# A third working tile for decoding packed weights on ScalarE, VectorE and GpSimd, in an FFT convolution with two MLP layers

## The chip, the cores and the metric

The kernel runs on one core of one Trainium2 chip. The metric is the device time of one execution in microseconds (us); for a set of runs, their median.

## What is computed

The input `x` (2 x 3008 x 256) is filtered along its 3008 time steps in the frequency domain, and the 6016 tokens that come out pass through two feed-forward layers, all in float32 accuracy:

```
X = np.fft.rfft(x, axis=1)
y = np.fft.irfft(X * (filt_r + 1j * filt_i)[None], n=3008, axis=1)
x = y.reshape(6016, 256)
g = x @ w_gate;  x = ((g / (1 + np.exp(-g))) * (x @ w_val)) @ w_out      # d_ff 1536
h = x @ w_in;    out = (h * np.clip(h + 3, 0, 6) / 6) @ w_out2           # d_ff 2048
```

The weights of the layers arrive as 64-bit words (`w1`, `w2`, the arrays `w_in` of the trace). The kernel itself turns them into float32, with integer and float operations on the two 32-bit halves of each word: this is the decoding.

## The kernel before

After the convolution the tokens are worked on in six blocks of up to 1024, each as two half blocks of 512 (or 480) columns. Layer 1 needs twelve units of work for a block (`F1` = 12), layer 2 eight (`G2` = 8). The main loop (`for s in range(S)`) runs over units: first the units of layer 1 for blocks 1 to 5, then those of layer 2 for all blocks. Matmuls of the first product of a unit write the banks `gv` (line 654); those of the second product, which need `hs`, write the banks `a` (line 699). In a unit of layer 1 TensorE executes 33 matmuls: seven products of three, and between them three groups of four of the second product of the unit before, which `fill()` hands out. Each float32 operand is split into a high part (a cast on ScalarE, line 687 for `hs`) and a low part (a subtraction on VectorE, line 116), and the second product multiplies those parts.

The order of instructions on every engine is the order in which the program writes them (`manual_schedule`). In a unit there are places, the spots N, A, B, T and C, at which extra work is put in by `add(unit, spot, step)`. So go:

- the weights of the unit after next: `split_unit` casts them on ScalarE (line 509) and subtracts on GpSimd (line 116, tiles `wu` and `wo`), from the stage tile `st`, which `ask_unit` loads (line 497);
- the next block's tokens: `plan_x` with loads `g` (line 141) or `raw` (line 740);
- the decoding of layer 2's weights, during layer 1's blocks 2 to 5: four steps q = 0 to 3 in each block, 16 in all, of 512 words a partition each.

A step of the decoding is an object of `Decode`. `ask_w2` loads its words into a tile `raw` (line 178) and `start` makes the tile `wa` with ScalarE's Abs of the high halves (line 183). `part` 0 to 4 run on VectorE (lines 192 to 202; part 1 makes the tile `ww`, part 4 is the last to read `raw`). `finish_w2` ends it on GpSimd: two additions of 256 columns (line 119), `ww` += `wa`, for every second step also four sums `sm`; one unit later the result goes to memory (lines 800 and 802). The places are dealt out of this list, five to a step, of which neighbours share one:

```
free_spots = [(u, name) for u in range(7) for name in "ABC" if (u, name) not in ((0, "B"), (1, "A"))]
...
places = [(s + u, name) for u, name in free_spots[4 * q:4 * q + 5]]
u, name = places[0]
add(u - 2, "N", ask_w2, g, i)
add(u - 1, "B", lambda g, i: dec2[g, i].start(), g, i)
```

The tiles of the decoding lie in the pool `late`, which has two buffers of a tag unless a tile asks for another number (`ww` asks for four). A tile of a tag takes over the place of the one that many allocations before it, and its first writer waits until the last user of that one is done. The pool is closed three units before layer 2 begins, and a pool of layer 2's tiles takes over its storage.

Of the kernel before, what the change touches and what calls it, by code (L numbers as in the profile page):

```python
# [9 lines left out]
F32 = mybir.dt.float32  # L10
# [6 lines left out]
P = 128  # L17
# [61 lines left out]
def fft_conv_glu_mlp(ctx: ExitStack, tc: tile.TileContext, x, filt, mats, sgn, w1, w2, out):  # L79
# [86 lines left out]
    class Decode:  # L166
# [12 lines left out]

        def start(self):  # L180
            if self.a is None:
                self.a = self.pool.tile([P, self.n], F32, tag="wa", name="wa")
            nc.scalar.activation(out=self.a, in_=self.raw[:, :, 1].bitcast(F32), func=AF.Abs)

        def part(self, i, engine=None):
# [77 lines left out]
    with tc.manual_schedule():  # L263
# [386 lines left out]
        def product(acc, s, a, i, start):  # L650
            k = units[s][0]
            n, w = half(k), wu[s][0]
            for q, (r, v) in enumerate(((0, 0), (0, 1), (1, 0))):
                nc.tensor.matmul(acc[:, :n], w[:, r, FORM[a] * P:(FORM[a] + 1) * P], xs_part(k, v, i),  # L654
                                 start=start and q == 0, stop=q == 2, skip_group_check=True)
# [160 lines left out]
        for k in range(2, n_block):  # L816
            s = F1 * (k - 1)
            for q in range(4):
                g, i = divmod(4 * (k - 2) + q, 2)
                places = [(s + u, name) for u, name in free_spots[4 * q:4 * q + 5]]  # L820
                u, name = places[0]
# [145 lines left out]
```

## Time and profile before

| | us |
|---|---|
| median of 3 runs | 1142.1 |
| lowest and highest run | 1141.64, 1144.41 |
| profiled execution | 1143.04 |
| its span, first to last instruction | 1141.2 |
| TensorE (PE) busy | 1119.2 (98%) |
| VectorE (DVE) busy | 853.5 (75%) |
| ScalarE (ACT) busy | 752.1 (66%) |
| GpSimd (POOL) busy | 598.0 (52%) |

The rows below are from the profiled execution. PEld is TensorE's loading of weights, which overlaps its matmuls; SPq is the queue of SyncE, which issues the DMAs. In a timeline a row may merge several instructions of a kind (x4); the time in brackets is how long the engine was idle before it, with the instruction that released it.

### The profile page before, as it was taken

To read this page: it belongs to the slowest core of one execution; us is meant where nothing else is said; L and a number is where in the kernel's file an instruction comes from. 1 tells how busy PE (TensorE), PEld (TensorE's weight loads), DVE (VectorE), ACT (ScalarE), POOL (GpSimd) and SP (SyncE) were. 2 spreads that over 40 slices of the span, in tenths; PEclk is the share of its full clock that TensorE was granted. 3 is DMA by queue.
4 is the path that set the end of the run, shared out by engine and by line. 5 is a ranking of instruction groups with operands and counts; after the bars stand their busy time and mean duration, and the time that the engine had idled before them with its cause. 6 is when DMAs were issued, how large, how long until landed. Compare 5 with 4: busy or idle time off the path is not lost.

```text
span 1141.2 us, 19170 instructions
## 1 busy us (share of the span) xinstructions
PE 1119.2 (98%) x7232; PEld 926.9 (81%) x7232; DVE 853.5 (75%) x1164; ACT 752.1 (66%) x1363; POOL 598.0 (52%) x779
## 2 busy tenths in 40 slices
PE   9999999999999999999999999999999999999998
PEld 7678887888788788878878888888888888888887
DVE  5889986668768777876877867768677677677765
ACT  4555447667567657756766777677677777777664
POOL 4752376755755765565567645444345444344440
PEclk9999999999999999999999999999999999999999
DMA  9964954732733462272354242322322412422200
GB/s 313 298 194 143 283 172 153 215 111 81 221 109 120 132 177 83 100 211 86 114 202 130 97 153 65 116 95 77 149 78 76 145 54 76 148 72 77 98 21 34
DMA packets 59484, 150.65 MB, mean 132 GB/s; under 512 B 5536, under 2 KB 27424, under 8 KB 57888
## 3 DMA queue, kind: packets, MB, share of 16 engines
q1 hardware_dynamic: 58848, 148.92, 40.4%
q8 instruction: 56, 0.92, 0.3%
q10 hardware_dynamic: 544, 0.52, 0.1%
q14 instruction: 36, 0.29, 0.1%
HBM read 117.17 MB, written 32.24 MB: 131 GB/s over the span
## 4 chain that ended last, share of the span: by engine, by line
PE 89%; DVE 3%; issue 2%; POOL 2%; DMA 2%; ACT 1%; SPq 1%; DVEq 0%
PE gv L654 42%; PE a L699 35%; PE gv L229 5%; PE a L237 2%; PE gv L370 1%; PE gv L156 1%; PE gv L328 1%; PE a L344 1%; POOL wu L116 1%; DMA ring<-x_in 1%; DVE h L681 1%; POOL ww L119 0%; DVE xs L116 0%; DMA w1f<-x 0%; DMA d<-turned 0%
## 5 line engine op out<-in xcount | busy, mean ns | idle before, releaser
L654 PE MATMUL gv<-xs,wu 128*128 128x512 f32 (+1 forms) x2268 | 572.2, 388 | 1.2 <-DVE h L593 0.8
L116 POOL TENSOR_TENSOR wu<-st,wu 128x224 fp32r<-128x224 f32 x432 | 311.6, 753 | 423.7 <-ACT wu L509 411.1
L654 PEld LDWEIGHTS gv<-xs,wu 128*128 128x128 f32 x2268 | 424.7, 189 | 87.7 <-DVE gv L119 3.4
L699 PE MATMUL a<-hs,wo 128*128 128x512 f32 (+1 forms) x1872 | 480.6, 387 | 10.4 <-ACT hs L687 10.4
L699 PEld LDWEIGHTS a<-hs,wo 128*128 128x128 f32 x1872 | 352.1, 188 | 79.1 <-ACT hs L687 12.6
L116 DVE TENSOR_TENSOR hs<-h,hs 128x1024 fp32r<-128x1024 f32 (+3 forms) x228 | 234.9, 1030 | 81.0 <-ACT hs L687 75.7
L687 ACT CAST hs<-h 128x512 fp32r<-128x512 f32 (+3 forms) x216 | 172.5, 799 | 132.2 <-DVE h L683 73.9
L116 POOL TENSOR_TENSOR wo<-st,wo 128x256 fp32r<-128x256 f32 x156 | 147.7, 959 | 0.0
L683 DVE SCALAR_TENSOR_TENSOR h<-h,gv 128x512 f32<-128x512 f32 (+1 forms) x144 | 96.4, 670 | 23.4 <-ACT h L677 23.0
L509 ACT CAST wu<-st 128x384 fp32r<-128x384 f32 x216 | 110.7, 563 | 0.6 <-DMA st<-w1f 0.6
L675 ACT ACTIVATE h<-gv 128x512 f32<-128x512 f32 (+1 forms) x120 | 70.6, 588 | 57.1 <-PE gv L654 56.8
L119 DVE TENSOR_TENSOR gv<-gv,h 128x512 f32<-128x512 f32 (+1 forms) x108 | 73.9, 685 | 43.7 <-PE gv L654 38.1
L677 ACT ACTIVATE h<-gv 128x512 f32<-128x512 f32 (+1 forms) x144 | 84.1, 584 | 16.2 <-PE gv L654 16.1
L119 DVE TENSOR_TENSOR h<-gv,h 128x512 f32<-128x512 f32 (+1 forms) x108 | 72.9, 675 | 25.7 <-PE gv L654 25.4
L862 ACT COPY gv<-gv 128x512 f32<-128x512 f32 (+1 forms) x108 | 60.9, 564 | 42.7 <-PE gv L654 39.1
L683 DVE SCALAR_TENSOR_TENSOR h<-h,h 128x512 f32<-128x512 f32 (+1 forms) x48 | 32.7, 681 | 59.4 <-ACT h L677 59.4
L866 ACT COPY h<-gv 128x512 f32<-128x512 f32 (+1 forms) x108 | 62.5, 579 | 15.8 <-PE gv L654 15.1
L681 DVE TENSOR_TENSOR h<-h 128x512 f32<-128x512 f32 (+1 forms) x60 | 61.2, 1020 | 1.9 <-ACT h L675 1.7
L116 DVE TENSOR_TENSOR xs<-raw,xs 128x512 fp32r<-128x512 f32 (+1 forms) x77 | 56.8, 739 | 0.1
L509 ACT CAST wo<-st 128x256 fp32r<-128x256 f32 (+1 forms) x108 | 54.2, 502 | 0.0
L552 ACT CAST xs<-raw 128x512 fp32r<-128x512 f32 (+1 forms) x77 | 45.7, 609 | 3.1 <-DVE raw L116 3.0
L229 PE MATMUL gv<-xs,wall_a 128*128 128x512 f32 x192 | 45.4, 391 | 0.0
(88 smaller groups left out, 893.7 us busy)
## 6 DMA issues: line engine op xcount, KB each, us to landing
st<-w1f SPq DMA_DIRECT2D x60, 576.0 KB, 4.3
st<-w2f SPq DMA_DIRECT2D x48, 704.0 KB, 4.0
raw<-w_in SPq DMA_DIRECT2D x16, 512.0 KB, 4.4
ring<-x_in SPq DMA_DIRECT2D x30, 256.0 KB, 5.3
x<-w_in SPq DMA_DIRECT2D x9, 768.0 KB, 5.5
d<-turned SPq DMA_DIRECT2D x32, 192.0 KB, 5.3
w1f<-x SPq DMA_DIRECT2D x12, 384.0 KB, 3.0
yd<-y SPq DMA_DIRECT2D x4, 1024.0 KB, 6.5
```

The lines of the kernel that those rows point to most:

```text
L116: (engine or nc.vector).tensor_tensor(out=out, in0=a, in1=b, op=ALU.subtract)
L119: (engine or nc.vector).tensor_tensor(out=out, in0=a, in1=b, op=ALU.add)
L229: nc.tensor.matmul(acc, w[:, r, c[k]:c[k] + P], xs[:, v, k], start=(r, v, k) == (0, 0, 0), stop=(r, k) == (1, 1))
L509: nc.scalar.copy(out=to[:, 0, at:at + hi - lo], in_=src[:, lo:hi])
L654: nc.tensor.matmul(acc[:, :n], w[:, r, FORM[a] * P:(FORM[a] + 1) * P], xs_part(k, v, i), start=start and q == 0, stop=q == 2, skip_group_c ...
L675: nc.scalar.activation(out=self.value(t, 0), in_=src, func=AF.Silu)
L677: nc.scalar.activation(out=self.value(t, a), in_=src, func=AF.Relu, bias=3.0)
L681: nc.vector.tensor_tensor(out=self.value(t, 0), in0=self.value(t, 0), in1=src, op=ALU.mult)
L683: nc.vector.scalar_tensor_tensor(out=self.value(t, a), in0=self.value(t, a), scalar=6.0, in1=src, op0=ALU.min, op1=ALU.mult)
L687: nc.scalar.copy(out=self.hs[:, t, :, 0, :self.n], in_=self.value(t))
L699: yield lambda t=t, v=v, a=a, j=j, r=r: nc.tensor.matmul(banks["a"][2 * j + t][:, :n], self.wo[:, r, (2 * a + j) * P:(2 * a + j + 1) * P], ...
L866: nc.scalar.copy(out=u.s7, in_=b3[:, :n])
```

## The change

The tag `wa` gets three buffers instead of two. It applies to the sixteen steps of layer 2's decoding; the decoding of layer 1's weights brings its own tile and does not come through this line.

```
         def start(self):
             if self.a is None:
-                self.a = self.pool.tile([P, self.n], F32, tag="wa", name="wa")
+                self.a = self.pool.tile([P, self.n], F32, tag="wa", name="wa", bufs=3)
             nc.scalar.activation(out=self.a, in_=self.raw[:, :, 1].bitcast(F32), func=AF.Abs)
```

No instruction is added, removed or moved. The pool grows by one tile of 512 float32, 2 KB a partition, and the tiles behind it lie 2 KB further on.

## Rows read from the trace of the kernel before

**Rows 1.** The page, part 1: busy time and share of the span.

```profile
PE 1119.2 (98%) x7232; PEld 926.9 (81%) x7232; DVE 853.5 (75%) x1164; ACT 752.1 (66%) x1363; POOL 598.0 (52%) x779
```

**Rows 2.** Waits of TensorE: waiter, released by: us in total, times, longest.

```profile
PE a L699 <- ACT hs L687: 10.4, 4, 2.6
```

**Rows 3.** Waits of all engines, the same columns.

```profile
ACT wa L183 <- POOL ww L119: 18.6, 4, 4.8
```

**Rows 4.** Timeline of ScalarE at sites 1 and 4: start, us, what.

```profile
302.00 0.66 ACT L183 ACTIVATE wa<-raw 128x512 f32<-128x512 f32 x1 [4.61 <-POOL ww L119]
302.57 0.57 ACT L687 CAST hs<-h 128x480 fp32r<-128x480 f32 x1
...
592.97 0.66 ACT L183 ACTIVATE wa<-raw 128x512 f32<-128x512 f32 x1 [4.60 <-POOL ww L119]
```

**Rows 5.** Timeline of GpSimd at site 1.

```profile
300.57 1.40 POOL L119 TENSOR_TENSOR ww<-ww,wa 128x256 f32<-128x256 f32 x2
```

**Rows 6.** Timeline of the DMA queue before sites 1 and 4.

```profile
294.84 0.33 SPq L178 DMA_DIRECT2D raw<-w_in  x1
...
585.82 0.33 SPq L178 DMA_DIRECT2D raw<-w_in  x1
```

**Rows 7.** DMAs: landing of site 1's load of raw; all sixteen of line 178.

```profile
raw<-w_in SPq DMA_DIRECT2D x1, 512.0 KB, 4.2
...
DMA to landing us min/median/max: 3.7/4.4/5.0
```

**Rows 8.** Timeline of TensorE: an undisturbed unit, site 1, site 4.

```profile
291.26 2.14 PE L654 MATMUL gv<-xs,wu 128*128 128x480 f32 x9
...
295.40 1.03 PE L699 MATMUL a<-hs,wo 128*128 128x480 f32 x4
...
298.44 2.12 PE L654 MATMUL gv<-xs,wu 128*128 128x480 f32 x9
303.19 1.97 PE L699 MATMUL a<-hs,wo 128*128 128x480 f32 x4 [2.64 <-ACT hs L687]
...
306.89 1.04 PE L699 MATMUL a<-hs,wo 128*128 128x480 f32 x4
...
589.40 2.12 PE L654 MATMUL gv<-xs,wu 128*128 128x480 f32 x9
...
596.50 1.03 PE L699 MATMUL a<-hs,wo 128*128 128x480 f32 x4
```

**Rows 9.** Timeline of TensorE's weight loads at site 1.

```profile
303.19 1.30 PEld L699 LDWEIGHTS a<-hs,wo 128*128 128x128 f32 x4 [3.05 <-ACT hs L687]
```

**Rows 10.** Cores: span, mean granted clock; windows: busy, PEclk, DMA share, GB/s.

```profile
core 0: 1141.2 us, clock 0.995
...
303.00:304.00 1.00, 0.81 (x2) 0.74 (x3) 0.82 (x2) 1.00 (x3) 1.00 (x3) 0.50 1.11 169
```

**Rows 11.** Timeline of TensorE at a shorter gap, and the window behind it.

```profile
176.62 1.65 PE L654 MATMUL gv<-xs,wu 128*128 128x512 f32 x6 [0.75 <-DVE h L593]
...
177.00:178.00 1.00, 1.00 (x6) 0.82 (x5) 0.32 (x1) 1.00 (x2) 0.18 (x1) 1.00 0.00 0
```

**Rows 12.** A stage load after site 1: issue, landing; ScalarE's cast, next hs.

```profile
299.02 0.40 SPq L497 DMA_DIRECT2D st<-w1f  x1
...
st<-w1f SPq DMA_DIRECT2D x1, 576.0 KB, 13.1
...
314.72 1.02 ACT L509 CAST wu<-st 128x384 fp32r<-128x384 f32 x2
317.65 0.59 ACT L687 CAST hs<-h 128x480 fp32r<-128x480 f32 x1 [1.61 <-DVE h L681]
```

**Rows 13.** Timelines: line 681 beside an idle and a busy GpSimd; a weight load.

```profile
271.17 0.68 DVE L681 TENSOR_TENSOR h<-h 128x512 f32<-128x512 f32 x1
292.99 1.19 DVE L681 TENSOR_TENSOR h<-h 128x480 f32<-128x480 f32 x1
...
288.98 1.17 PEld L654 LDWEIGHTS gv<-xs,wu 128*128 128x128 f32 x6 [0.50 <-DVE gv L119]
```

More of the change, by code (lines that the diff above doesn't have):

```diff
@@ L181, in start @@
             if self.a is None:
-                self.a = self.pool.tile([P, self.n], F32, tag="wa", name="wa")
+                self.a = self.pool.tile([P, self.n], F32, tag="wa", name="wa", bufs=3)
             nc.scalar.activation(out=self.a, in_=self.raw[:, :, 1].bitcast(F32), func=AF.Abs)
```

## Prediction, before the change was run

> **What bounds the kernel now.** I read the page first: TensorE is busy for 1119.2 us of a span of 1141.2 us [rows 1], so an edit pays only if it closes one of TensorE's gaps or changes its speed. Then the list of TensorE's waits alone: almost all of its recorded idle time after the start is one line, 10.4 us in 4 waits of at most 2.6 us, the second-layer matmuls of line 699 waiting for ScalarE's cast `hs` of line 687 [rows 2]. Then the waits of all engines: ScalarE waits 18.6 us, also in 4 places, for GpSimd: its Abs of line 183, which writes a new `wa`, stands until GpSimd has done with `ww` at line 119 [rows 3]. The timeline joins the two. At 302.00 us the Abs starts after 4.61 us of idling, so ScalarE had been free since 297.39; the cast `hs` follows at 302.57 [rows 4]; and at 303.19 TensorE starts again after 2.64 us [rows 8]. What released the Abs is the pair of GpSimd additions that starts at 300.57 and takes 1.40 us, to 301.97 [rows 5].
>
> The code says why. Each of the sixteen decoding steps takes a `wa` tile; with two tiles, step m needs the tile of step m-2, and that is free when the last part of step m-2, the addition of line 119, is done. In a block of twelve units the four steps q = 0 to 3 start in unit -1, 1, 2 and 3 (spot B), and finish in units 2 (A), 3 (B), 4 (C) and 6 (A). Step 3 starts in the very spot in which step 1 finishes, one instruction behind it in the program, while GpSimd has a whole unit's split queued ahead of that finish. That is one stall in each of four blocks, which is the count in both lists. Sites 1 and 4 stand in the rows; the other two repeat them.
>
> **What a site costs.** TensorE's order around a site is nine matmuls (S4 of this unit, 00 and S3 of the next), four of line 699, six of line 654, and the next four. From the first of the nine to the second group of four are 19 matmuls. Undisturbed that is 295.40 - 291.26 = 4.14 us; at site 1 it is 306.89 - 298.44 = 8.45 us; at site 4, 596.50 - 589.40 = 7.10 us [rows 8]. So site 1 costs 4.31 us and site 4 costs 2.96 us. The idle time is nearly the same; the rest of site 1 is the clock: after the gap the granted clock reads 0.50, the lower of the two levels [rows 10]. For the whole kernel: the mean granted clock of 0.995 is 0.005 x 1141.2 = 5.7 us lost [rows 10], and with 10.4 us of idling [rows 2] that makes 16.1 us. By sites, three like the first and one like the fourth give 15.9. I take **16.0 us** as what goes if the four stalls go whole.
>
> **The change, part by part.** (1) A third `wa`: step m now needs the tile of step m-3. For step 3 that is step 0, whose addition was issued in unit 2; for steps 0, 1 and 2 it is a step of the block before. ScalarE's wait for GpSimd at line 183 has nothing left to wait for. (2) Nothing is added to any queue: no operation, no DMA and no operand changes, so the added work is nothing. The 2 KB a partition shift the `ww` tiles behind `wa`; that storage is used again only by tiles of the last stage, three units after the decoding ends, and I cost it at nothing; without that cover a wait would show there on first use. (3) What ScalarE waits for next. The Abs also reads `raw`, which has two tiles and stays so. The load for step 3 is issued at 294.84, when step 1 has left its `raw` [rows 6], and lands 4.2 us later [rows 7]: 299.04. So ScalarE still idles, from 297.39 to about 299.1, but 2.9 us less than to 302.00. At site 4 the same reading, issue at 585.82 and Abs at 592.97 [rows 4, 6], gives 590.02 and 2.95 us.
>
> Does that clear TensorE? The cast follows the Abs by 0.57 us and TensorE's weights are loaded 0.62 us after the cast starts [rows 4, 9]: 299.1 + 1.19 = 300.3. The weight load would have gone at 303.19 - 3.05 = 300.14 [rows 9], the matmul at 303.19 - 2.64 = 300.55 [rows 8]. So the load is some 0.15 us late and the matmul is not, by a margin of 0.26 us. **The stall is not removed with room to spare, it is cut to where it just no longer shows.** If `raw` lands after 5.0 us, the longest of the sixteen [rows 7], instead of 4.2, a gap of 0.54 us stays; that is one bound, and zero is the other. A gap of that size has a neighbour in the trace: 0.75 us at 176.62, after which the clock reads 1.00 [rows 11], so I do not add a clock loss to it.
>
> (4) VectorE and GpSimd get closer together. VectorE stands still during the stall, while GpSimd works; without it both work. VectorE's product at line 681 takes 0.68 us when GpSimd is idle and 1.19 us when GpSimd works beside it, and where the decoding is dense the weight load behind VectorE's sum waits 0.50 us [rows 13]. One such wait is likely in the unit after each site. I take 0.4 us a site for (3) and (4) together, nearest to the 0.50 of that row, with bounds of zero and 0.54 + 0.50 = 1.04 us. A gain beyond the 16.0 us I exclude, since the matmuls themselves are untouched.
>
> The Trainium skill has a rule that speaks against the change here ("SBUF — State Buffer", section "Who interferes with whom"): a VectorE instruction with two SBUF inputs and a GpSimd instruction that reads SBUF take a shared port in turn, and the second is blocked for the whole of the first. The two durations of line 681 agree with it in kind. By that rule alone three of VectorE's products in the unit would each be held, which is the third rival below.
>
> (5) The transfers that the stall covered. The load of the stage tile issued at 299.02 lands 13.1 us later, at 312.1; its cast starts at 314.72 now and would be due at 314.72 - 4.31 = 310.4 [rows 12]. ScalarE will then wait for this DMA for some 1.7 us. Behind that cast ScalarE idles for 1.61 us in any case before its next `hs` [rows 12], so the wait takes the place of that idle time, and I cost it at nothing (0.1 us at most); without that cover each microsecond of landing later is one of TensorE, if TensorE has no slack of its own there.
>
> **Sum.** Profiled execution: 1143.04 - 16.0 + 4 x 0.4 = 1128.6 us. It stands 0.9 us above the median of the runs, so 1142.1 - 14.4 = **1127.7 us**.
>
> **Rivals.** *The stall comes back as a wait for `raw`.* For it: the margin is 0.26 us, and the load cannot be issued earlier, since step 1 holds its tile. Against it: the landing would have to reach 5.0 us at all four sites. Price: a gap of 0.54 us and the 0.50 of (4) at each site, and should the clock fall again, as at three of four sites now, 5.7 us: 1142.1 - 16.0 + 4.2 + 5.7 = 1136 us.
>
> *Nothing changes.* If the Abs were held by something other than the tile of step 1, the third tile would do nothing: 1142 us. Against it: the Abs starts 0.03 us behind the end of GpSimd's pair [rows 4, 5], and the other input landed 3 us earlier.
>
> *VectorE becomes the bound beside GpSimd.* Three of its products in the unit after a site are stretched by 1.19 - 0.68 = 0.51 us each [rows 13], with no slack ahead of TensorE: 1.5 us a site, 1142.1 - 16.0 + 6.1 = 1132 us. The dense units of now show 0.50 us, not 1.5.
>
> *Slower than before, by the stage loads.* If the DMA queues, without the pauses, fall behind, ScalarE's cast of the stage tile holds the next `hs`, and TensorE. Today's landing of 13.1 us is covered by what (5) names. From a landing of about 17 us (13.1 and the 4.0 of gain) a site loses more than it gains; at 20 us it loses 6.9 us and the clock's 4.31 - 2.96 = 1.35 us, against the 4.0 us gained. With three sites so, 1142.1 + 3 x 4.25 - 4.0 = 1151 us. For it: 13.1 us is three times the landing of `raw` a few microseconds earlier, so the queues are full there. Against it: no byte is added, and the same transfers start at the same moments up to the site.
>
> **How the numbers follow.** The forecast has a chance of 0.82, the return of the wait for `raw` 0.05, VectorE as the bound 0.07, no change 0.04, slower 0.02. All but the last two are faster by over 0.3% (about what a measurement of this kernel can tell from no change, 3.4 us): 0.94; within it 0.04; slower 0.02. The low end is the fastest run with nothing left over, 1141.64 - 16.0 = 1125.6, less 1.35 us if the clock fell at all four sites there: 1124. The high end takes in the upper bound of (3) and (4) with a clock loss at half of the sites, 1142.1 - 16.0 + 4.2 + 2.8 = 1133, and the third rival: 1133.5.
>
> **What would show it.** Right: ScalarE's wait for GpSimd at line 183 is gone, and in its place stand four waits of up to 1.8 us for the DMA of `raw`; the 10.4 us of TensorE on `hs` are under 2; the mean granted clock is 1.00; the casts of line 509 show a few waits for `st`. Wrong: TensorE still waits on line 687 in four places, for over half a microsecond each; or its waits on VectorE's sums of line 119 grow by over a microsecond a site; or the clock stays at 0.995 without the gaps, which would mean that the gaps were not what lowered it.

## The result, and the profile after

With three tiles the kernel takes 1132.0 us (median of 5 runs, 1129.3 to 1133.45) against 1142.33 us before (5 runs, the three of the table above among them): a ratio of 0.9901, with a 95% interval of 0.9883 to 0.9919. It is faster by 10.3 us between the medians, 11.3 us by the ratio; 14.4 us were forecast. The profiled execution took 1130.35 us (span 1128.6), against 1143.04 (span 1141.2) before.

First some of the waits of all engines after the change (waiter, released by: us in total, times, longest):

```profile
ACT wu L509 <- DMA st<-w1f: 6.3, 6, 2.2
ACT wa L183 <- DMA raw<-w_in: 6.2, 4, 1.8
PEld gv L654 <- DVE gv L119: 5.9, 11, 0.8
PEld a L699 <- ACT hs L687: 1.7, 5, 0.5
```

and one of them before it:

```profile
PEld gv L654 <- DVE gv L119: 3.4, 8, 0.6
```

ScalarE's 18.6 us at line 183 for GpSimd [rows 3] are gone. In their place stand four waits for the load of `raw`, at most 1.8 us, and waits for stage tiles, where one of 0.6 us stood before. TensorE's matmuls no longer wait for the cast `hs` at all [rows 2]; only its weight loads do, for 1.7 us. The last line but one after the change shows the new cost: weight loads wait 5.9 us for VectorE's sum of line 119, in 11 places, where they waited 3.4 us in 8 places before.

Site 1 after the change, ScalarE's timeline and then TensorE's (start, duration, what, idle time before it and what ended it):

```profile
299.51 0.67 ACT L183 ACTIVATE wa<-raw 128x512 f32<-128x512 f32 x1 [1.84 <-DMA raw<-w_in]
300.09 0.58 ACT L687 CAST hs<-h 128x480 fp32r<-128x480 f32 x1
```

```profile
298.71 2.12 PE L654 MATMUL gv<-xs,wu 128*128 128x480 f32 x9
300.72 1.13 PE L699 MATMUL a<-hs,wo 128*128 128x480 f32 x4
...
303.05 1.03 PE L699 MATMUL a<-hs,wo 128*128 128x480 f32 x4
...
306.31 2.16 PE L654 MATMUL gv<-xs,wu 128*128 128x480 f32 x9
...
310.47 1.37 PE L699 MATMUL a<-hs,wo 128*128 128x480 f32 x4
312.24 1.57 PE L654 MATMUL gv<-xs,wu 128*128 128x480 f32 x6 [0.40 <-DVE gv L119]
...
314.51 2.11 PE L654 MATMUL gv<-xs,wu 128*128 128x480 f32 x9
```

and from before, behind site 1, TensorE's next two groups of nine and a weight load:

```profile
309.94 2.11 PE L654 MATMUL gv<-xs,wu 128*128 128x480 f32 x9
...
315.18 1.17 PEld L654 LDWEIGHTS gv<-xs,wu 128*128 128x128 f32 x6 [0.50 <-DVE gv L119]
...
317.45 2.11 PE L654 MATMUL gv<-xs,wu 128*128 128x480 f32 x9
```

The Abs starts 4.39 us after the issue of its load at 295.12; the cast follows at once, and TensorE goes on at 300.72 without a gap. The 19 matmuls of the site take 303.05 - 298.71 = 4.34 us, against 8.45 with the stall and 4.14 undisturbed [rows 8]. What is left comes for the most part a unit later: four matmuls that undisturbed take 0.87 us take 312.24 - 310.47 = 1.77 us. Two of their weight loads wait 0.47 us for a cast `hs` that itself waited for VectorE's product of line 681, and the loads behind them wait 0.80 us for VectorE's sum.

Whole units show it too, from one group of nine to the next. Undisturbed a unit takes 298.44 - 291.26 = 7.18 us [rows 8]. Before the change the site's unit took 309.94 - 298.44 = 11.50 us and the unit behind it 317.45 - 309.94 = 7.51 us, with a wait of 0.50 us for VectorE's sum in it; after the change they take 306.31 - 298.71 = 7.60 us and 314.51 - 306.31 = 8.20 us. Timed at all four sites from each unit's first matmul, against an undisturbed unit of the same block, the two units lost 17.4 us before and lose 4.4 us after. Of these 4.4 us, 1.4 us are lost in the sites' units and 3.0 us in the units behind them, where 1.3 us were lost before the change as well. The mean granted clock is 1.000, against 0.995 [rows 10].

VectorE and GpSimd in the same stretch:

```profile
300.70 0.70 DVE L116 TENSOR_TENSOR hs<-h,hs 128x480 fp32r<-128x480 f32 x1 [1.04 <-ACT hs L687]
301.32 1.19 DVE L681 TENSOR_TENSOR h<-h 128x480 f32<-128x480 f32 x1
302.43 0.96 DVE L200 TENSOR_SCALAR wa<-ww 128x512 uint32<-128x512 uint32 x1
303.31 0.65 DVE L119 TENSOR_TENSOR gv<-gv,h 128x480 f32<-128x480 f32 x1
...
306.12 0.64 DVE L681 TENSOR_TENSOR h<-h,gv 128x480 f32<-128x480 f32 x1
```

```profile
300.84 2.27 POOL L119 TENSOR_TENSOR ww<-ww,wa 128x256 f32<-128x256 f32 x2
...
305.91 2.92 POOL L116 TENSOR_TENSOR wu<-st,wu 128x224 fp32r<-128x224 f32 x4
```

and line 200 at site 1 before the change, when GpSimd had just finished:

```profile
304.73 0.41 DVE L200 TENSOR_SCALAR wa<-ww 128x512 uint32<-128x512 uint32 x1
```

VectorE first stands 1.04 us, because the cast is late by the wait for `raw`. Then it runs without a pause, beside a GpSimd that works too: the part of line 200 takes 0.96 us instead of 0.41, and GpSimd's pair of additions 2.27 us instead of the 1.40 of [rows 5], when VectorE stood still.

### The profile page after: what moved, and what is told of

The parts are those of the page before. It is cut to its first block, busy times and chain, and to the rows that moved or that the text cites. A ratio compares the mean times of both kernels' runs of the same rounds, so it can differ in the third digit from the quotient of the medians.

```text
span 1128.6 us, 19174 instructions
## 1 busy us (share of the span) xinstructions
PE 1115.5 (99%) x7232; PEld 923.3 (82%) x7232; DVE 861.4 (76%) x1164; ACT 751.2 (67%) x1363; POOL 606.3 (54%) x779
## 4 chain that ended last, share of the span: by engine, by line
PE 84%; DVE 8%; DMA 4%; ACT 2%; issue 2%; SPq 0%; POOL 0%; ACTq 0%; DVEq 0%
PE gv L654 39%; PE a L699 33%; PE gv L229 5%; PE a L237 2%; DVE h L681 2%; DVE hs L116 2%; DMA raw<-w_in 1%; PE gv L156 1%; PE gv L370 1%; PE a L344 1%; PE gv L328 1%; ACT hs L687 1%; DMA d<-turned 1%; DVE gv L119 1%; DMA x<-w_in 1%
```

## Where the time is measured

Executions of one kernel differ by up to 0.6% here. In the profiled executions most of that lies ahead of the sites. It is visible in ScalarE's first instruction of line 675, at the start of the main loop; the two rows are of before and after:

```profile
180.58 0.60 ACT L675 ACTIVATE h<-gv 128x512 f32<-128x512 f32 x1 [1.62 <-PE gv L654]
```

```profile
180.89 0.60 ACT L675 ACTIVATE h<-gv 128x512 f32<-128x512 f32 x1 [1.62 <-PE gv L654]
```

Over all the profiled executions this start lies between 179.98 and 184.95 us, whatever the kernel, though no instruction in front of it was changed. So beside the ratio I give for each kernel the **main loop**: the span less this start, in its profiled execution. Before: 1141.2 - 180.58 = 960.6 us; after: 1128.6 - 180.89 = 947.7 us, which is 12.9 us less. Each ratio is taken against runs of the kernel before that were made together with it. All nine experiments:

| kernel | wa, raw tiles | ratio to before, 95% interval | span - start = main loop, us |
|---|---|---|---|
| before | 2, 2 | | 1141.2 - 180.58 = 960.6 |
| e1: raw alone | 2, 3 | 1.0004, 0.9988 to 1.0019 | 1143.2 - 182.47 = 960.7 |
| e5: filled gaps | 2, 2 | 0.9967, 0.9953 to 0.9981 | 1136.6 - 180.14 = 956.5 |
| e4: two sites | 2 and an own one, 2 | (one run) | 1138.9 - 184.95 = 954.0 |
| the change | 3, 2 | 0.9901, 0.9883 to 0.9919 | 1128.6 - 180.89 = 947.7 |
| the change again | 3, 2 | 0.9902, 0.9881 to 0.9923 | 1131.3 - 183.02 = 948.3 |
| e2: both | 3, 3 | 0.9878, 0.9856 to 0.9900 | 1126.4 - 180.99 = 945.4 |
| e3: later Abs | 2, 2 | 0.9870, 0.9847 to 0.9893 | 1125.2 - 179.98 = 945.2 |
| e7: later Abs | 3, 2 | 0.9879, 0.9855 to 0.9902 | 1128.4 - 183.34 = 945.1 |
| e8: e7, addition on VectorE | 3, 2 | 0.9873, 0.9849 to 0.9898 | 1128.4 - 182.98 = 945.4 |
| e6: the change without GpSimd's part | 3, 2 | 0.9845, 0.9821 to 0.9870 | 1122.0 - 180.04 = 942.0 |

## The experiments

**Is it the tile `wa`, or the input `raw`? (e1)** The Abs needs both, and both have two buffers.

```
-            self.raw, self.a, self.w = place or (pool.tile([P, n, 2], U32, tag="raw", name="raw"), None, None)
+            self.raw, self.a, self.w = place or (pool.tile([P, n, 2], U32, tag="raw", name="raw", bufs=3), None, None)
```

> Two wa tiles as before, but three raw tiles, so that step 3's words are loaded earlier. Theory (the Abs is held by the tile wa of step 1 until GpSimd's addition): the four waits of ScalarE for GpSimd at line 183 stay at 4.6 to 4.8 us and TensorE's four at 2.5 to 2.6 us, time within 0.3% of before (1139 to 1146 us). Rival (the Abs is held by its input raw): the four waits go and the time falls to about 1130 us.

The load now goes out at 286.28 us, and yet site 1's Abs waits as before:

```profile
303.82 0.67 ACT L183 ACTIVATE wa<-raw 128x512 f32<-128x512 f32 x1 [4.58 <-POOL ww L119]
```

The ratio is 1.0004. The input was not what held the Abs; the rival falls.

**Does each site cost on its own? (e4)** Step 3 of the first two blocks gets a tile of its own, the rest keep two.

```
             dec2[g, i] = Decode(pool["late"], w2[:, g, 1024 * i:1024 * (i + 1)].unsqueeze(1), 512)
+            if 2 * g + i in (3, 7):
+                dec2[g, i].a = pool["late"].tile([P, 512], F32, tag="wb", name="wb", bufs=1)
```

> Two wa tiles, but step 3 of the first two of the four blocks has a tile of its own. Read from the first ScalarE instruction of line 675 to the end, which leaves the first 180 us out (960.6 us with two tiles, 947.7 with three). Theory (each site costs on its own, and the first two give back 3.2 and 4.1 us in the changed kernel): two waits of line 699 on line 687 instead of four, about 5.2 us instead of 10.4, and 953.3 us. Rival (sites depend on each other): under 950 or over 957 us.

```profile
PE a L699 <- ACT hs L687: 5.3, 2, 2.6
```

Two waits are left, 5.3 us, and the main loop takes 954.0 us where 953.3 was expected. In this one execution each site costs on its own, as the theory had it; the time lies in neither of the rival's ranges.

**Is it a matter of tiles, or of order? (e3)** Two tiles as before; the Abs of step 3 stands further on, in spot A of the next unit, behind two casts `hs` that it stood ahead of.

```
-                add(u - 1, "B", lambda g, i: dec2[g, i].start(), g, i)
+                add(*((u, "A") if q == 3 else (u - 1, "B")), lambda g, i: dec2[g, i].start(), g, i)
```

> Two wa tiles and two raw tiles as before; step 3's Abs is moved from spot B of unit 3 to spot A of unit 4, about 4 us later in the order of ScalarE and still ahead of VectorE's first part in spot C. Theory (the stall is the order: the Abs stands ahead of the cast hs while its tile is not free): the cast no longer stands behind the wait, TensorE's four waits go, ScalarE idles less than 1 us at line 183, and the time is that of three tiles or up to 4 us better: 1126 to 1131 us. Rival (only a third tile helps, since step 1's addition is late for the later place too): waits of over 1 us at line 183 and 1135 us or more.

```profile
ACT wa L183 <- POOL ww L119: 3.5, 4, 0.9
```

ScalarE still waits for the same tile, but at most 0.9 us, at a place where `hs` is already cast, and TensorE has no wait on it. The main loop takes 945.2 us, 2.5 us less than with the third tile, and needs no storage. The expectation of under 1 us at line 183 holds for each site.

**What is left at the sites: the wait for `raw`? (e2)** Three tiles of each kind (the two edits together).

> Three wa tiles and three raw tiles. Theory (the 4.4 us that TensorE still loses at the four sites in the changed kernel begin with ScalarE's wait for raw, 6.2 us in all, which leaves VectorE idle for 1.0 us at site 1 and late for a unit and a half): the waits of line 183 for the DMA go, and 2 to 4 us with them: 1126 to 1129 us in a profiled execution against 1130.35. Rival (VectorE beside GpSimd is what is short there, whenever the Abs starts): 1129 to 1133 us, as with three wa alone.

```profile
297.66 0.67 ACT L183 ACTIVATE wa<-raw 128x512 f32<-128x512 f32 x1
298.89 0.59 ACT L687 CAST hs<-h 128x480 fp32r<-128x480 f32 x1 [0.56 <-DVE h L681]
```

No wait is left at line 183, and the cast `hs` comes 0.56 us after ScalarE was free for it, held by VectorE now. The main loop loses 2.3 us against the change (945.4 from 947.7), at the lower end of what the theory asked for. The earlier load and the later Abs come to the same: both end the lateness that the wait for `raw` had put on the cast.

**Is VectorE short because of GpSimd? (e6)** The change, with GpSimd's part of the decoding left out (TensorE then reads weights that are not finished).

```
-                formed["w2", g] = new_sums()
-                weight_sums(formed["w2", g], *(w[:, c * P:(c + 1) * P] for c in range(4)), nc.gpsimd)
+                formed["w2", g] = w[:, :512].rearrange("p (s c) -> p s c", c=P)
...
-            for q in (0, 256):
-                plus(w[:, q:q + 256], w[:, q:q + 256], a[:, q:q + 256], nc.gpsimd)
```

> Three wa tiles; GpSimd's part of layer 2's decoding is left out: the two additions that end a step and the four sums of every second step (so layer 2's weights are not exact). VectorE and ScalarE do all that they did. Theory (VectorE is short at the sites because GpSimd's work beside it stretches its products from 0.65 to 1.19 us): VectorE is some 2 us less busy, TensorE's waits on VectorE's sums at the sites halve, and 1 to 2.5 us go. Rival (the wait for raw alone makes the leftover): the time stays within 0.7 us of the changed kernel.

Part 1 of the page, after the change and without GpSimd's part:

```profile
PE 1115.5 (99%) x7232; PEld 923.3 (82%) x7232; DVE 861.4 (76%) x1164; ACT 751.2 (67%) x1363; POOL 606.3 (54%) x779
```

```profile
PE 1111.4 (99%) x7232; PEld 924.2 (82%) x7232; DVE 845.6 (75%) x1164; ACT 752.7 (67%) x1363; POOL 550.6 (49%) x715
```

and two of its waits:

```profile
ACT wa L183 <- DMA raw<-w_in: 4.4, 4, 1.5
PEld gv L654 <- DVE gv L119: 0.2, 1, 0.2
```

The same 1164 instructions of VectorE take 15.8 us less, eight times what I had expected, and TensorE's loads wait 0.2 us for it instead of 5.9. The main loop takes 942.0 us: 5.7 us less than the change, where 1 to 2.5 us had been expected. By the units, 4.4 of the 5.7 us are all that the sites still lost, the 1.3 us that they had lost before the change included; the other 1.3 us come from the unit two ahead of each site, whose wait of 0.50 us in [rows 13] stood there before and after. ScalarE still waits 4.4 us for `raw` (6.2 with GpSimd's part), and here it costs nothing. So the two causes are one chain: a late cast costs TensorE only where VectorE has no slack to make it up, and VectorE has none because GpSimd works beside it. The rival falls.

**Both cures together (e7), and the addition on VectorE (e8).** First the change with the later Abs of e3; then the same with the addition moved from GpSimd to VectorE.

> Three wa tiles, and step 3's Abs in spot A of unit 4 instead of spot B of unit 3. Theory (what is left at the sites is VectorE beside GpSimd, which neither edit touches; ScalarE's last waits of 0.9 us for GpSimd are off the path): the waits at line 183 go, and from the first line 675 to the end it takes 944.5 to 945.4 us, as with the moved Abs alone (945.2). Rival (those 0.9 us hold TensorE too): 942 to 944 us.

> As the kernel before it in this call, with the addition that ends a step on VectorE, one of 512 columns, instead of two of 256 on GpSimd; GpSimd keeps the sums. Theory (beside GpSimd's additions VectorE loses about as much as the addition itself costs it, 0.68 us, 16 times): 944 to 947 us from the first line 675 to the end. Rival (the additions on GpSimd cost VectorE much more than that): 942 to 943.5 us.

945.1 and 945.4 us: a third tile adds nothing to the later Abs, and the addition on VectorE costs it about what it saves (VectorE is busy for 860.7 us in e7 and 861.4 us in e8). Both came as the theory had them. By the ratios the later Abs (0.9870) and the two together (0.9879, 0.9873) lie below the change, with overlapping intervals; the 2.5 us are read from the main loops.

**What did the clock cost? (e5)** The kernel before, with a product repeated four times where TensorE stood still.

```
-            product(b1, s, "00", 0, True)
+            for _ in range(5 if s in (16, 28, 40, 52) else 1):
+                product(b1, s, "00", 0, True)
```

> The kernel before, two wa tiles, with the first product of units 16, 28, 40 and 52 issued five times instead of once: 12 more matmuls, about 2.6 us, that stand in TensorE's order exactly where it waits at the four sites; the repeats give the same values. Theory (the granted clock falls because TensorE stood still for 2.5 us): ScalarE's waits at line 183 stay, TensorE's gaps are under 0.3 us, the mean granted clock is 1.00, and the time is that of before less the 5.7 us of the clock: 1136 to 1138 us. Rival (the clock falls at these places for another reason): clock 0.995 and 1141 to 1144 us.

TensorE's timeline at site 1, and a window that in the kernel before reads 0.50 [rows 10] (busy time of the engines, clock, DMA share, GB/s):

```profile
298.01 4.71 PE L654 MATMUL gv<-xs,wu 128*128 128x480 f32 x21
302.81 1.14 PE L699 MATMUL a<-hs,wo 128*128 128x480 f32 x4
...
305.15 1.03 PE L699 MATMUL a<-hs,wo 128*128 128x480 f32 x4
...
303.00:304.00 1.00, 1.00 (x5) 0.75 (x5) 1.00 (x2) 1.00 (x3) 0.90 (x2) 1.00 1.16 169
```

ScalarE waits as before (18.7 us), the site is as long up to the restart (4.80 us from the nine to the four, 4.75 before), but the clock stays up and the ten matmuls behind it take 305.15 - 302.81 = 2.34 us instead of 306.89 - 303.19 = 3.70 [rows 8]. The ratio 0.9967 is clear of 1; the median of 1140.5 us lies above the 1136 to 1138 us expected. In the main loop it is 4.1 us, of the 5.7 that I had put down to the clock. The sites say where the difference lies. With the clock up, site 1 takes 305.15 - 298.01 = 7.14 us from the nine to the second four, 3.00 us more than undisturbed; that is what site 4 cost with its 2.96 us [rows 8], and 1.31 us less than site 1 before. So a standstill costs about 3.0 us a site, not only its 2.6 us of idling, and the clock about 1.3 us at three of the sites: 4 x 3.0 + 3 x 1.31 = 15.9 us. The mean clock of the kernel before also holds a low stretch (0.50 from 1139.2 to 1141.2) at its end, behind the last matmul, which costs nothing.

**Where do executions differ?** The change again, profiled a second time.

> The changed kernel once more, three wa tiles. Theory: the four sites cost TensorE 4 to 5 us in every execution, and what makes the executions differ by 4 us (1129.3 to 1133.45) lies elsewhere, in the first 100 us, where TensorE waits on DMA and issue by 4 to 6 us. Rival: the sites themselves differ from execution to execution, by over 2 us in sum.

Its main loop is 0.6 us longer than that of the first execution (948.3 to 947.7), its start 2.1 us later (183.02 to 180.89). There TensorE waits for a load of `g`, 1.67 us, and the clock of the window behind it reads 0.50:

```profile
71.43 0.39 PE L156 MATMUL a<-mat,g 48*64 48x47 f32 x2 [1.67 <-DMA g<-d]
...
72.00:78.00 6.00, 5.69 (x66) 3.81 (x67) 3.52 (x5) 1.94 (x4) 0.00 (x0) 0.50 0.66 217
```

In the first execution of the change the same place shows 0.17 and 0.52 us of waiting and a clock of 1.00. So 2.1 of the 2.7 us between the two spans lie ahead of the main loop, and the rival falls: the sites lose 4.4 us in the first of these executions and 5.1 us in the second.

## Why the prediction was right, and where its size was off

- **The bound and the cause** were right. The two lists of waits, joined by the timeline, named the tile; e1 and e4 show that it was the tile and that each site counts alone. The shifted storage of part (2) cost nothing: from the first matmul of layer 2's units to the end both profiles take 490.6 us.
- **The cost of a site**, 16.0 us in all, was right as a sum: against undisturbed units the four sites' units lost 16.1 us. Its parts were not those of the prediction. 10.4 us of idling went whole, but a standstill costs about 3.0 us a site, 12 us in all, and the clock 4.1 us by e5, not 5.7. The two errors, 1.6 us each, cancel; the sum held because it was also reckoned by sites.
- **What ScalarE waits for next** was right: `raw`, four times, up to 1.84 us at site 1 (1.7 expected), and TensorE's matmuls show no gap behind it. The margin of 0.26 us held.
- **The mis-sized term is (3) and (4), what is left over.** I put 0.4 us a site on it, from the one wait of 0.50 us in [rows 13]. Measured in the main loop it is 16.0 - 12.9 = 3.1 us, 0.8 us a site, inside the bounds (zero to 1.04) but twice the value taken. A wait of 0.50 us behind site 1 stood there before the change (at 315.18), so that it could not be the price of the change. The error was to take ScalarE's lateness and VectorE's fullness as two small terms of their own. They work in series: the late cast empties VectorE for 1.04 us just before a unit and a half in which GpSimd's work leaves it no slack, and TensorE pays for most of it a unit later. e2 and e3 take the lateness away and get 2.3 to 2.5 us back; e6 takes the fullness away and gets all 4.4 us of the sites back, with most of the lateness still there.
- **The third rival**, VectorE as the bound beside GpSimd, was given 0.07 and 1132 us, which is the median measured. The number agrees in part by chance: its profiled execution would have been 1143.04 - 16.0 + 6.1 = 1133.1 us, and 1130.35 was measured, between it and the 1128.6 of the forecast. But its mechanism is what e6 confirms, at about half of its price of 1.5 us a site. The sign of being wrong that belongs to it, a growth of over a microsecond a site in the waits on VectorE's sums, did not come: they grew by 2.5 us at four sites.
- **The rule on the shared port** that I weighed (the Trainium skill, "SBUF — State Buffer", section "Who interferes with whom") is borne out in kind by e6: with less of GpSimd's work, VectorE's unchanged instructions take 15.8 us less. Line 681 fits it as well: beside a busy GpSimd it takes 1.19 us with both inputs in SBUF, where the tiles lie (`h<-h`, at 301.32) and 0.64 us with one of them in a matmul bank (`h<-h,gv`, at 306.12). The section also names `tensor_scalar` in a two-port mode, as line 200 may be: 0.96 us at the site, 0.41 without GpSimd beside it. No run here shows which instruction blocks which.
- **The stage loads** cost nothing, as in (5): ScalarE waits 6.3 us for them, and e2, with 0.6 us of such waits, and e7, with 6.7 us, have the same main loop (945.4 and 945.1 us). At site 1 the cast that I expected to wait 1.7 us waited 0.19 us, since it came due later than I had reckoned; the longest of the waits, 2.2 us, stood at another site. The rival on the slower side did not occur.
- **From the profile to the median** the forecast lost another 2.6 us. The profiled execution came to 1130.35 us where 1128.6 was expected, 1.5 us of that from the term above and 0.3 us from the start. But I had placed the median 0.9 us below the profile, as before, and it lies 1.65 us above. Executions differ by as much in the start of the main loop, ahead of the change, but the executions without a profile do not show their start, so that this is not shown for the median; a difference of a profile from a median of three runs should have widened the range, not shifted the forecast.

## What to carry to other kernels

When an engine's wait is released by the last user of a rotating tile, count the allocations: one more buffer removes it, but placing the waiting instruction behind the work that others need can do as much without storage, as e3 shows here. Before costing the gain, ask what the second input of the waiting instruction is, when it lands, and whether the engine behind it has slack to make up what remains. A stall also separates engines that disturb each other; some of what its removal gains is lost again when they meet.

## What the runs showed of the hardware

A standstill of TensorE can cost its clock as well, but does not every time. At site 1 a gap of 2.64 us is followed by a granted clock of 0.50, the lower of the two levels [rows 8, 10]. At site 4 as long a gap is not; the rows are TensorE's restart and the window behind it (busy time, clock, DMA share, GB/s), in the kernel before:

```profile
594.16 1.14 PE L699 MATMUL a<-hs,wo 128*128 128x480 f32 x4 [2.64 <-ACT hs L687]
...
594.00:595.00 1.00, 0.84 (x4) 0.68 (x4) 0.86 (x2) 1.00 (x4) 1.00 (x3) 1.00 1.08 418
```

Ahead of the main loop, gaps of 1.67 and 0.49 us were followed by 0.50 in one execution of the change, and in e4, with 1.54 and 0.51 us of idling at the same place, the clock read 1.00:

```profile
75.19 0.31 PE L156 MATMUL a<-mat,g 48*64 48x47 f32 x2 [1.54 <-DMA g<-d]
...
72.00:78.00 6.00, 3.95 (x124) 2.85 (x114) 2.94 (x5) 2.04 (x5) 2.87 (x4) 1.00 0.83 208
```

What decides it, no run here shows. Filling the gaps with matmuls whose results were not needed kept the clock up and made the kernel before faster by 0.3%.

GpSimd's adds and VectorE's arithmetic slow each other here: leaving out some 56 us of GpSimd's busy time (606.3 to 550.6) freed 15.8 us on VectorE, though no instruction of VectorE was changed.
